# Gate tiles 4 to 7 as one quad ahead of the first attention-output pair, then two pairs per gate pair

## The chip, the cores and the metric

The kernel runs on one core of one Trainium2 chip. The metric is the device time of one execution in microseconds; the median of the executions is quoted, with the lowest and the highest. Every run carries a state (fast or slow) and the mean clock granted to TensorE.

## The reference

One block over 2048 tokens of width 448 computes a linear attention and an MLP from the same normalised input, and multiplies them:

```python
xn = layernorm(x)
# A: linear attention, 16 heads of 28; pq, pk = phi(q), phi(k)
kv  = einsum("bhsd,bhse->bhde", pk, v);  z = einsum("bhsd->bhd", pk)
num = einsum("bhqd,bhde->bhqe", pq, kv)
den = einsum("bhqd,bhd->bhq", pq, z)[..., None] + 1e-6
s   = (num / den) @ wo
# B: MLP with 1792 hidden units
h = relu(xn @ w1 + b1) ** 2
g = silu(h @ w2 + b2)
out = x + s * g
```

## The kernel before

The program lists its operations; a small list scheduler fixes the order on DVE, ACT and the buffers, while TensorE (PE) keeps the order of the program. Only its last stage matters here. It has two kinds of output tile of 128 tokens x 448:

- a **g tile** (`gg`): the second matmul of the MLP, 14 contraction chunks. DVE adds the bias, ACT applies silu;
- an **S tile** (`ss`): the attention output, 4 contraction chunks, from the scaled queries `pqT`, `pqR` and a folded weight `msb`. DVE multiplies it by the gate, POOL adds the residual, a DMA stores it.

Most of these tiles run in pairs. One tile of a pair uses the upper 64 contraction rows of the array, the other the lower 64, at the same time; then they swap rows. `phase` issues one such half. The fourth chunk of an S tile has 64 rows only (448 = 3 x 128 + 64), so the first half of an S pair is 8 matmuls (`K4`, four per tile) and the second 6 (`K3`).

```python
def phase(lo, hi):                 # lo on array rows 0-63, hi on rows 64-127, interleaved
    ...
    op = add("pe", f, reads + [u.bank for u in us if u.op], [u.bank for u in us], dur)
    for h, (u, ks) in enumerate((lo, hi)):
        if ks:
            if u.op and u.half != h:
                op.sync.add(u.op)  # the same bank from the other rows: wait until those have drained
            u.op, u.half = op, h
# ... cut ...
def scale_q():                     # 1/den goes to DRAM and back, broadcast over partitions into rb, rbR
    # ... cut: the DMAs ...
    for g in range(NG):            # DVE, four groups of 512 tokens; the first serves S tiles 0 to 3
        add("dve", lambda e, _, sl=sl: e.tensor_tensor(out=pqT[sl], in0=pqT[sl], in1=rb[sl], op=ALU.mult), ...)
        add("dve", lambda e, _, c=c: e.tensor_tensor(out=pqR[:, c], in0=pqR[:, c], in1=rbR[:, c], op=ALU.mult), ...)
# ... cut ...
full(gg(0)); full(gg(1)); z_heads(); token_sum(0); den(); open_gates(); scale_q()
token_sum(3); token_sum(1); token_sum(2); full(gg(2)); fold_wv(); full(gg(3))
for r in range(4): fold_wo(r)
C = range(0, NF)
for i, *pairs in ((4, 0), (6, 2), (8, 4, 6), (10, 8), (12, 10, 12)):   # g pair, S pair(s)
    ga, gb = gg(i), gg(i + 1)
    us = [(ss(j), ss(j + 1)) for j in pairs]
    phase((ga, C), (gb, C))
    x, y = us[0]
    if len(us) == 1:
        phase((x, K4), (y, K4)); phase((gb, C), (ga, C)); phase((y, K3), (x, K3))
    else:
        v, w = us[1]
        phase((x, K4), (y, K4)); phase((gb, C), (ga, C)); phase((v, K4), (w, K4))
        phase((y, K3), (x, K3)); phase((w, K3), (v, K3))
full(gg(14)); ...                  # the last two tiles, cut finer
```

## Time and profile before

| | before |
|---|---|
| time, median of the first 3 runs | 143.47 us (143.3 to 143.54) |
| span of the profiled run, granted clock | 142.0 us, 1.00 |
| PE, DVE, ACT, POOL busy | 97%, 64%, 55%, 17% |
| the stretch that the change edits | 96.4 to 132.4 us |

From the page of the kernel before, the busy time of each engine (us, share of the span, instructions):

```profile
PE 137.8 (97%) x1215; PEld 67.4 (47%) x1215; DVE 91.3 (64%) x218; ACT 78.7 (55%) x151; POOL 23.4 (17%) x37
```

One row of its table of windows, for the edited stretch. The columns are length, then busy time and instructions of PE, weight loads, DVE, ACT and POOL, then granted clock, DMA share and GB/s:

```profile
96.40:132.40 36.00, 36.00 (x380) 18.57 (x380) 17.35 (x34) 6.51 (x12) 10.05 (x10) 1.00 0.11 34
```

The whole list of what PE waited for (total, times, longest, in us):

```profile
PE pb L1010 <- DVE junk L345: 1.3, 1, 1.3
PE pb L487 <- DVE xn L466: 0.2, 1, 0.2
```

PE is busy 36.00 of 36.00 us in the stretch, and both of its waits belong to the first six microseconds. A busy PE need not be at its peak, so the chain of work that ended last is read too (start, length, line and number of matmuls; L905 is g, L971 is S):

```profile
96.51 2.76 PE pb L905 x28
99.27 0.76 PE pb L971 x8
100.03 2.65 PE pb L905 x28
102.67 0.57 PE pb L971 x6
103.24 2.65 PE pb L905 x28
105.89 0.76 PE pb L971 x8
...
132.37 2.75 PE pb L905 x14
```

A g half is 28 matmuls in two concurrent row halves, so 14 slots: 2.65 / 14 = 0.189 us each. The Trainium skill ("TensorE: Matmul & The Clock Gate", Back-to-back issue gap) gives N/2.4 + 2.5 ns as the gap from one matmul to the next on a warm array, which is 189 ns for 448 columns. It adds that in a sustained stream the formula is too high for many columns (about 131 ns measured for 512). That is not so in this trace, where sustained streams of 448 columns run at the formula's 189 ns, so the stretch is taken to run at the issue rate.

What the first S pair depends on, from the timeline of DVE (start, length, engine, line), and then the S pair itself, from the timeline of PE:

```profile
97.32 0.96 DVE L866 TENSOR_TENSOR pqT<-pqT,xT 128x1536 bf16<-128x1536 bf16 x1
98.19 0.28 DVE L872 TENSOR_TENSOR pqR<-pqR,xT 128x256 bf16<-128x256 bf16 x1
```

```profile
96.45 2.82 PE L905 MATMUL pb<-w,r 64*128 64x448 bf16 x28
99.11 0.35 PE L971 MATMUL pb<-msb,pqR 64*128 64x448 bf16 x2
```

The scaled block is ready at 98.47 us (98.19 + 0.28), 1.15 us after its first multiply began. The S pair starts at 99.11, when the g half before it has been issued (96.45 + 2.65). So it does not wait, but it has only 0.64 us to spare.

### The profile page before, as it was taken

To read this page: it belongs to the slowest core of one execution; us is meant where nothing else is said; L and a number is where in the kernel's file an instruction comes from. 1 tells how busy PE (TensorE), PEld (TensorE's weight loads), DVE (VectorE), ACT (ScalarE), POOL (GpSimd) and SP (SyncE) were. 2 spreads that over 40 slices of the span, in tenths; PEclk is the share of its full clock that TensorE was granted. 3 is DMA by queue.
4 is the path that set the end of the run, shared out by engine and by line. 5 is a ranking of instruction groups with operands and counts; after the bars stand their busy time and mean duration, and the time that the engine had idled before them with its cause. 6 is when DMAs were issued, how large, how long until landed. Compare 5 with 4: busy or idle time off the path is not lost.

```text
span 142.0 us, 3024 instructions
## 1 busy us (share of the span) xinstructions
PE 137.8 (97%) x1215; PEld 67.4 (47%) x1215; DVE 91.3 (64%) x218; ACT 78.7 (55%) x151; POOL 23.4 (17%) x37
## 2 busy tenths in 40 slices
PE   6999999999999999999999999999999999999992
PEld 2344444444444444444445455654555555555482
DVE  0979698698897999678959900149852436052743
ACT  2667979889878898879799572323030211030220
POOL 6000000000000000000790000000050507350670
DMA  4997768999250300000000025891001110201022
GB/s 111 329 334 225 78 176 279 342 244 129 55 64 15 74 19 5 0 9 14 0 0 0 0 78 135 186 166 32 5 6 58 37 32 32 97 27 43 32 97 67
DMA packets 19809, 12.90 MB, mean 91 GB/s; under 512 B 9364, under 2 KB 19412, under 8 KB 19796
## 3 DMA queue, kind: packets, MB, share of 16 engines
q1 hardware_dynamic: 17644, 11.22, 32.5%
q10 hardware_dynamic: 2152, 1.50, 4.8%
q8 instruction: 9, 0.15, 0.4%
q14 instruction: 4, 0.03, 0.1%
HBM read 8.78 MB, written 2.10 MB: 77 GB/s over the span
## 4 chain that ended last, share of the span: by engine, by line
PE 93%; DVE 3%; DMA 2%; issue 0%; DVEq 0%
PE pb L905 30%; PE pb L640 30%; PE pb L597 8%; PE pb L971 8%; PE pb L672 6%; PE pb L628 6%; DMA x_tok<-in_A_x_dram 2%; DVE st L444 1%; PE pb L678 1%; PE pb L765 1%; PE pb L726 1%; PE pb L487 1%; PE pb L803 0%; DVE xn L466 0%; PE pb L488 0%; DVE xT L497 0%
## 5 line engine op out<-in xcount | busy, mean ns | idle before, releaser
L640 PE MATMUL pb<-xT,w 64*128 64x512 bf16 x392 | 50.8, 376 | 0.1
L905 PE MATMUL pb<-w,r 64*128 64x448 bf16 (+3 forms) x378 | 45.1, 343 | 0.0
L649 ACT ACTIVATE r<-pb,b1f 128x512 bf16<-128x512 f32 x56 | 34.9, 689 | 4.1 <-PE pb L640 4.1
L640 PEld LDWEIGHTS pb<-xT,w 64*128 64x128 bf16 x392 | 21.4, 94 | 23.3 <-ACT r L649 0.6
L905 PEld LDWEIGHTS pb<-w,r 64*128 64x128 bf16 (+1 forms) x378 | 22.9, 95 | 19.9 <-issue 1.2
L916 DVE TENSOR_TENSOR gbuf<-pb,b2b 128x448 bf16<-128x448 f32 (+1 forms) x16 | 9.3, 609 | 33.2 <-PE pb L905 33.2
L881 ACT ACTIVATE gbuf<-gbuf 128x448 bf16<-128x448 bf16 (+1 forms) x16 | 8.6, 565 | 36.2 <-DVE gbuf L916 34.4
L950 POOL TENSOR_TENSOR xn<-xn,x_tok 128x448 bf16<-128x448 bf16 x15 | 15.1, 1029 | 48.7 <-DVE xn L941 48.7
L597 PE MATMUL pb<-w_qkv,xT 64*128 64x512 bf16 (+1 forms) x106 | 17.6, 377 | 0.0
L628 PE MATMUL pb<-xT,w_qkv 64*128 64x512 bf16 x84 | 15.5, 376 | 0.0
L657 DVE TENSOR_TENSOR r<-r 128x512 bf16<-128x512 bf16 x38 | 13.2, 418 | 0.0
L382 POOL MEMSET kvm<- 128x2048 bf16 x1 | 1.8, 1804 | 65.0 <-DVE zb L622 65.0
L971 PE MATMUL pb<-msb,pqT 64*128 64x448 bf16 (+3 forms) x93 | 11.2, 343 | 0.0
L444 DVE BATCH_NORM_STATS2 st<-x_tok 128x6 f32<-128x448 bf16 x16 | 9.4, 612 | 2.4 <-DMA x_tok<-in_A_x_dram 2.4
L575 ACT ACTIVATE qk<-pb 128x512 bf16<-128x512 f32 x16 | 9.0, 594 | 3.3 <-PE pb L597 2.7
L585 DVE SCALAR_TENSOR_TENSOR qk<-pb,qk 128x512 bf16<-128x512 f32 x16 | 10.7, 686 | 0.2
L941 DVE TENSOR_TENSOR xn<-pb,gbuf 128x448 bf16<-128x448 f32 (+2 forms) x17 | 9.3, 590 | 1.9 <-ACT gbuf L881 1.5
L658 ACT ACTIVATE r<-r 128x512 bf16<-128x512 bf16 x18 | 10.4, 651 | 0.0
L597 PEld LDWEIGHTS pb<-w_qkv,xT 64*128 64x128 bf16 (+1 forms) x106 | 6.6, 94 | 6.5 <-DVE xT L497 0.3
L672 PE MATMUL pb<-qk,xn 128*128 128x448 bf16 x48 | 9.4, 353 | 0.0
L628 PEld LDWEIGHTS pb<-xT,w_qkv 64*128 64x128 bf16 x84 | 6.0, 94 | 5.0
L616 DVE TENSOR_TENSOR zacc<-zacc,qk 128x448 f32<-128x448 f32 x13 | 8.1, 622 | 0.3
(81 smaller groups left out, 98.6 us busy)
## 6 DMA issues: line engine op xcount, KB each, us to landing
out_dram<-xn SPq DMA_DIRECT2D x15, 112.0 KB, 1.7
w<-in_B_w_dram SPq DMA_DIRECT2D x1, 1568.0 KB, 9.7
x_tok<-in_A_x_dram SPq DMA_DIRECT2D x3, 448.0 KB, 4.4
w<-in_B_w_dram SPq DMA_DIRECT2D x2, 384.0 KB, 4.7
xT<-rows ACTq DMA_DIRECT2D x6, 112.0 KB
w<-in_B_w_dram SPq DMA_DIRECT2D x1, 576.0 KB, 5.3
xT<-rows SPq DMA_DIRECT2D x5, 112.0 KB
w_o<-in_A_wo_dram SPq DMA_DIRECT2D x1, 392.0 KB, 10.9
```

The costliest lines, as they stand in the source:

```text
L444: "dve", lambda e, _: e.bn_stats(st6[:, si, :], x_tok[:, si, :]), [("x", si)], [("st", si)], 0.553
L585: lambda e, _: e.scalar_tensor_tensor(out=slot, in0=src(), scalar=1.0 + 1e-6, in1=slot, op0=ALU.add, op1=ALU.max),
L597: return e.matmul(ps(b)[:, 0:512], xT[half[h], c, si * P : (si + 1) * P], w_qkv[half[h], c, 384 : 2 * D], start=start, stop=stop,)
L628: return e.matmul(ps(b)[:, 0:512], w_qkv[half[h], c, m * P : (m + 1) * P], xT[half[h], c, g * 512 : (g + 1) * 512], start=start, stop=stop,)
L640: return e.matmul(ps(b)[:, 0:512], w_1[half[h], c, fi * P : (fi + 1) * P], xT[half[h], c, g * 512 : (g + 1) * 512], start=start, stop=stop,)
L649: lambda e, _: e.activation(out=slot, in_=ps(b)[:, 0:512], func=AF.Relu, bias=b1f[:, fi : fi + 1]),
L657: return e.tensor_tensor(out=slot, in0=slot, in1=slot, op=ALU.mult)
L658: return e.activation(out=slot, in_=slot, func=AF.Square)
L672: last = e.matmul(ps(b)[:, 0:D], xn[:, si, c * P : (c + 1) * P], pk_of(si), start=(si == 0), stop=(si == NT - 1),)
L905: return e.matmul(ps(b)[:, 0:n], r2[half[h], fi, si * P : (si + 1) * P], w_2[half[h], fi, c], start=start, stop=stop)
L950: eng, lambda e, _: e.tensor_tensor(out=ob, in0=ob, in1=x_tok[:, si, c], op=ALU.add),
L971: return e.matmul(ps(b)[:, 0:n], q, m, start=start, stop=stop)
```

## The change

The intent is to put more matmul work between the folded weights and the first S pair, so that the latter has no need to wait for the scaled queries. Two g pairs now go first, each filling the time in which the other drains. The S pairs that are displaced are caught up at two per g pair. The last group, and all that follows it, is the same in both.

```diff
-        for i, *pairs in ((4, 0), (6, 2), (8, 4, 6), (10, 8), (12, 10, 12)):
+        def s_pair(j):
+            x, y = ss(j), ss(j + 1)
+            return lambda: phase((x, K4), (y, K4)), lambda: phase((y, K3), (x, K3))
+
+        g4, g5, g6, g7 = (gg(i) for i in range(4, 8))
+        s0 = s_pair(0)
+        phase((g4, C), (g5, C))
+        phase((g6, C), (g7, C))
+        phase((g5, C), (g4, C))
+        s0[0]()
+        phase((g7, C), (g6, C))
+        s0[1]()
+        for i, *pairs in ((8, 2, 4), (10, 6, 8), (12, 10, 12)):
             ga, gb = gg(i), gg(i + 1)
-            us = [(ss(j), ss(j + 1)) for j in pairs]
+            us = [s_pair(j) for j in pairs]
             phase((ga, C), (gb, C))
-            ...
+            us[0][0]()
+            phase((gb, C), (ga, C))
+            for u, v in zip(us, us[1:]):
+                v[0]()
+                u[1]()
+            us[-1][1]()
```

More of the change, by code (lines that the diff above doesn't have):

```diff
@@ L1092, in bass_recurrent_scan__linear_attn_block__dense_activation_squared_relu__prompt_kernel @@
         C = range(0, NF)
-        for i, *pairs in ((4, 0), (6, 2), (8, 4, 6), (10, 8), (12, 10, 12)):
+        def s_pair(j):
[10 more added lines that the diff above has]
+        for i, *pairs in ((8, 2, 4), (10, 6, 8), (12, 10, 12)):
             ga, gb = gg(i), gg(i + 1)
-            us = [(ss(j), ss(j + 1)) for j in pairs]
+            us = [s_pair(j) for j in pairs]
             phase((ga, C), (gb, C))
-            x, y = us[0]
-            if len(us) == 1:
-                phase((x, K4), (y, K4))
-                phase((gb, C), (ga, C))
-                phase((y, K3), (x, K3))
-            else:
-                v, w = us[1]
-                phase((x, K4), (y, K4))
-                phase((gb, C), (ga, C))
-                phase((v, K4), (w, K4))
-                phase((y, K3), (x, K3))
-                phase((w, K3), (v, K3))
+            us[0][0]()
[4 more added lines that the diff above has]
+            us[-1][1]()
         full(gg(14))
```

## The prediction

> What bounds the kernel. TensorE, and nothing else is close: the page has PE busy 97% of a 142.0 us span at granted clock 1.00, DVE 64%, ACT 55%. The table of waits has only two for PE, 1.3 and 0.2 us, both at the very start. In the stretch that the change edits, 96.4 to 132.4 us, PE is busy 36.0 of 36.0 us, DVE 17.4, POOL 10.1, ACT 6.5. The chain of work that ended last stays on PE from 84.9 to 139.4 us; a tail of about 2.5 us (DVE, store) follows.
>
> What the change does. It adds and removes no work. The instruction order by engine shows the same half-row matmuls in the stretch with some S blocks later; ACT and SP keep their order; DVE's gate additions and S multiplies interleave differently; from g pair 12 on everything is as it was, so the tail is untouched. PE pieces from the chain: a g half is 2.65 us (28 matmuls in two concurrent row halves, 14 x 0.189), an S half 0.76 (8) or 0.57 (6). Before: three groups of 2.65+0.76+2.65+0.57 = 6.63 and two of 7.95 with a second S pair, together 35.8. After: the quad 4 x 2.65 + 0.76 + 0.57 = 11.9 and three groups of 7.95, together 35.8. The Trainium skill ("TensorE: Matmul & The Clock Gate", Back-to-back issue gap) gives N/2.4 + 2.5 ns for warm matmuls, 189 ns at 448 columns; the trace agrees (2.65/14). This stretch already runs at issue rate; reordering cannot compress it.
>
> What it could buy. The first S pair needs the first scaled query block (DVE, 97.32 to 98.47 us, itself behind the reciprocal's broadcast DMAs). It starts at 99.11, exactly when the g half before it ends: no wait, about 0.6 us to spare. After the change it should start near 104.4, with about 6 us to spare. That is insurance against a late broadcast, not time; the three runs lie within 0.24 us, so I see no execution in which it would pay much.
>
> What it could cost. The quad's second g pair takes the banks of the folded-weight blocks, evicted by 97.2 us and wanted at 99.1: no stall. A g pair's second half waits for its first half's drain; one phase of at least 0.76 us lies between, as today. The later groups use the pattern that 8:(4,6) and 12:(10,12) run today, 1.89 us for the last 20 S matmuls (10 x 0.189), no stall. DVE per 7.95 us group: two additions and four multiplies, about 3.5 us; POOL four residuals, 4.0 us. Gate buffers wrap every eight tiles: S 0 and 1 finish near 110 us, gates 8 and 9 are written after about 114. Stores come later but none at the end. All of it hides behind PE.
>
> Prediction: 143.4 us, 8 in 10 between 143.1 and 143.8; faster by over 2%: 0.01, within 2%: 0.98, slower by over 2%: 0.01.
>
> What would show it. Span within 0.3 us of 142.0; PE 36.0 busy of 36.0 in the stretch; four 2.65 us g halves with S first at about 104.4 us; no new PE wait in the table of waits; final chain as before.
>
> What would make it wrong: the broadcast landing later in unprofiled runs than in the trace (then up to some tenths faster); a bank held longer than I read for g 6, g 8 or S 4 (some tenths slower each); two phases of one bank too close; or a granted clock below 1.00.

## The result, and the profile after

| | before | after |
|---|---|---|
| median, same rounds | 143.39 us (143.25 to 143.54, 6 runs) | 143.51 us (143.27 to 143.8, 6 runs) |
| span of the profiled run, clock | 142.0 us, 1.00 | 142.2 us, 1.00 |

The ratio is 1.0009 with a 95% interval of 0.9993 to 1.0025: the same. Ratios here and below are the mean time of one kernel's fast runs over that of the other's fast runs of the same rounds, so they are not quite the ratio of the medians quoted. Executions over 1.5% slower than the fastest of the same kernel are left out of the means. Faster or slower needs 2%. A smaller difference counts as the same; where the text takes one for real, its interval leaves out 1.

The lines of after that answer to those of before, in the same order: the page's busy times, the row of windows, and the whole list of PE's waits.

```profile
PE 138.2 (97%) x1215; PEld 67.7 (48%) x1215; DVE 91.4 (64%) x218; ACT 78.7 (55%) x151; POOL 23.4 (16%) x37
```

```profile
96.40:132.40 36.00, 36.00 (x380) 18.53 (x378) 17.42 (x33) 6.50 (x12) 10.02 (x10) 1.00 0.11 35
```

```profile
PE pb L1010 <- DVE junk L345: 1.2, 1, 1.2
```

The chain of work that ended last, after:

```profile
96.68 8.05 PE pb L905 x84
104.73 0.76 PE pb L971 x8
105.49 2.65 PE pb L905 x28
108.14 0.57 PE pb L971 x6
108.70 2.65 PE pb L905 x28
111.35 0.76 PE pb L971 x8
112.11 2.65 PE pb L905 x28
114.76 1.89 PE pb L971 x20
...
132.54 2.75 PE pb L905 x14
```

The pieces are the same, in another order. From the first g half to the full-row tile that follows the stretch it takes 132.37 - 96.51 = 35.86 us before and 132.54 - 96.68 = 35.86 us after. No new wait appeared; the only one that is gone, 0.2 us on L487, lies in the first six microseconds.

The timelines of DVE and then of PE around the first S pair, after:

```profile
97.73 0.96 DVE L866 TENSOR_TENSOR pqT<-pqT,xT 128x1536 bf16<-128x1536 bf16 x1 [0.39 <-DMA xT<-rows]
98.61 0.28 DVE L872 TENSOR_TENSOR pqR<-pqR,xT 128x256 bf16<-128x256 bf16 x1
```

```profile
96.61 8.12 PE L905 MATMUL pb<-w,r 64*128 64x448 bf16 x84
104.57 0.35 PE L971 MATMUL pb<-msb,pqR 64*128 64x448 bf16 x2
```

The block is ready at 98.89 us and the S pair starts at 104.57, so it has 5.7 us to spare. In this execution DVE waited 0.39 us for the broadcast (the bracket); the old order would still have had 0.4 us left.

Before the changed code is reached, after is already 0.17 us late (96.68 against 96.51), which is the difference between the two spans (142.0 and 142.2). The first PE rows of the timelines, before and then after:

```profile
1.25 4.09 PE L1010 MATMUL pb<-junk 128*128 128x512 bf16 x10 [1.25 <-DVE junk L345]
5.52 0.34 PE L487 MATMUL pb<-ident,xn 128*128 128x128 bf16 x3 [0.18 <-DVE xn L466]
```

```profile
1.25 4.45 PE L1010 MATMUL pb<-junk 128*128 128x512 bf16 x10 [1.25 <-DVE junk L345]
5.55 0.50 PE L487 MATMUL pb<-ident,xn 128*128 128x128 bf16 x3
```

The ten warm-up matmuls and the first transposes, which both programs have, ran slower in this execution (0.50 instead of 0.34 us for three transposes), and everything after them is shifted. The change has no part in it: the slower start (4.45 and 0.50 us) is also in the trace of b_late2, which has the old order, and the faster one (3.93 and 0.34) in that of a_tok3, which has the new.

### The profile page after: what moved, and what is told of

It reads as the page before. It is cut to its first block, busy times and chain, and to the rows that moved or that the text cites. A ratio compares the mean times of both kernels' runs of the same rounds, so it can differ in the third digit from the quotient of the medians.

```text
span 142.2 us, 3026 instructions
## 1 busy us (share of the span) xinstructions
PE 138.2 (97%) x1215; PEld 67.7 (48%) x1215; DVE 91.4 (64%) x218; ACT 78.7 (55%) x151; POOL 23.4 (16%) x37
## 4 chain that ended last, share of the span: by engine, by line
PE 97%; DVE 1%; issue 0%; DVEq 0%
PE pb L905 30%; PE pb L640 30%; PE pb L597 8%; PE pb L971 8%; PE pb L672 6%; PE pb L628 6%; PE pb L1010 3%; PE pb L678 1%; PE pb L765 1%; PE pb L487 1%; PE pb L726 1%; PE pb L488 1%; PE pb L803 0%; DVE xT L497 0%; DVE xn L941 0%
```

## The experiments

The theory: PE's issue rate alone sets the time of the stretch, and the change only moves the point at which a late scaled block starts to cost. One rival: the first S pair was never near critical. Another: the null result is a gain at the first S pair that is lost again to the denser S work. A third: the small differences between the runs of the two are the change's own cost. Twelve kernels ran.

### A late scaled block, before and after

The scaled block is made late by N dummy multiplies on DVE, directly ahead of the first scaling. They write into buffers that are dead by then, so the results stay correct, and no other instruction changes its place.

```diff
+            def pads(e, g):
+                for i in range(N if g == 0 else 0):
+                    w = (w_1 if i < 4 else qk)[:, :, :].rearrange("p a b -> p (a b)")   # dead here
+                    e.tensor_tensor(out=w[:, ...1536 columns of its own...], in0=rb[:, :, 0:512], in1=rb[:, :, 0:512], op=ALU.mult)
 ...
-   lambda e, _, sl=sl: e.tensor_tensor(out=pqT[sl], in0=pqT[sl], in1=rb[sl], op=ALU.mult)
+   lambda e, _, sl=sl, g=g: pads(e, g) or e.tensor_tensor(out=pqT[sl], in0=pqT[sl], in1=rb[sl], op=ALU.mult)
```

**Before with two (b_late2).** 

> Before, with two dummy multiplies of 128x1536 (0.87 us apart in the trace) put ahead of the first query scaling on DVE, so that the first scaled block comes about 1.75 us later; nothing else moves. Theory (PE-bound stretch, first S pair with 0.4 to 0.6 us to spare): PE idles about 1.1 to 1.4 us before the first S pair and the time rises by as much, 144.5 to 144.9 us. Rival (the first S pair is not near critical, something else sets the time): no change.

Measured: 144.71 us (144.67 to 144.74) against 143.57; ratio 1.0077 (1.0056 to 1.0098), about +1.1 us. The PE timeline shows where:

```profile
96.63 2.82 PE L914 MATMUL pb<-w,r 64*128 64x448 bf16 x28
100.53 0.36 PE L980 MATMUL pb<-msb,pqR 64*128 64x448 bf16 x2 [1.07 <-DVE pqR L881]
```

The rival that the first S pair is not near critical falls: about 1.75 us of added lateness cost 1.1 us, so about 0.6 us was absorbed.

**Before with four (b_late4).** 

> Before with four dummy multiplies, about 3.5 us. Theory: PE idles 2.9 to 3.1 us at the first S pair, time 146.3 to 146.6 us; 1.75 us more than with two. Rival: no change, or less than 1 us.

Measured: 147.83 us (146.85 to 147.91); ratio 1.0279 (1.0242 to 1.0316), about +4.0 us. PE idled 2.74 us, nearly as expected, but the time rose by over a microsecond more than either theory said. The expectation was missed, and the chain shows by what:

```profile
102.03 0.93 PE pb L980 x8
102.97 4.33 PE pb L914 x28
```

The g half after the stall took 4.33 us instead of 2.65. That is followed up below.

**After with four (a_late4).** 

> After with the same four dummy multiplies. Theory: the first S pair starts at about 104.5 us and its block is ready near 102.4 us, so no PE wait and 143.5 us, the same as after without them (within 0.3 us). Rival (the change's later S pairs are only just served, its null result is a gain and a loss that cancel): 0.5 us or more slower.

Measured: 143.27 us (143.25 to 143.43); ratio to the kernel before 0.9979 (0.9961 to 0.9997). The DVE row of the dummies and the PE rows:

```profile
98.14 3.57 DVE L866 TENSOR_TENSOR w<-xT 128x1536 bf16<-128x1536 bf16 x4 [1.01 <-DMA xT<-rows]
```

```profile
96.40 8.12 PE L914 MATMUL pb<-w,r 64*128 64x448 bf16 x84
104.36 0.35 PE L980 MATMUL pb<-msb,pqR 64*128 64x448 bf16 x2
```

With the same dummies that cost before 4.0 us, after loses nothing. The broadcast also came late by itself here: DVE waited 1.01 us for it. Without the dummies the block would have been ready at 98.14 + 1.15 = 99.29 us, while the first g half was issued by 96.40 + 2.65 = 99.05. By this arithmetic the old order would have waited about 0.2 us in this execution.

**After with eight (a_late8).** 

> After with eight dummy multiplies, about 7.0 us, just past the spare time. Theory: block ready near 105.8 us, PE idles 1.0 to 1.5 us at the first S pair, time 144.5 to 145.0 us; so the change moved the point where a late block costs from 0.5 to about 5.7 us. Rival: costs far more than 1.5 us, because DVE work piles up behind the late scaling and holds the banks.

Measured: the three fast runs took 144.95, 145.39 and 145.69 us; ratio 1.0121 (1.009 to 1.0152), about +1.7 us. The fourth, which was the profiled one, took 147.52 us and counts as slow. The cost is somewhat over the range expected but well short of the 7 us added, so a late block costs in the new order too, only some 5 us later. The profile of the slow run shows one thing that precedes its stall: the broadcast landed at 98.92 us, 1.79 us after DVE was ready for it. PE then idled 2.57 us, and the granted clock was 0.50 from 107 to 110 us. Runs of b_late4 in which the clock fell count as fast, since that kernel has no much faster run beside them; so the 1.7 us here, without such a run, and the 4.0 us there are not quite like for like. Why the three fast runs lie up to 0.7 us above the expected range is not known, as none of them was profiled.

### Why four dummies cost more than the stall

**Before with three (b_late3).** 

> Before with three dummy multiplies, between the two that cost their stall alone (1.1 us) and the four that cost 4.3 us, of which 1.7 us was the g half after the stall at half the granted clock. Theory A (a stall costs its length, and the clock falls only from some idle time between 1.1 and 2.7 us on): either 145.4 to 145.9 us with clock 1.00, or about 147.0 us with the clock down, or some of each. Theory B (the extra of the four was not the clock but DVE piling up behind): 146.2 us, in proportion, clock 1.00.

Measured: 147.22, 145.91, 147.45 and 147.82 us, with mean granted clocks of 0.988, 1.000, 0.987 and 0.988. The ratio is 1.0246 (1.0188 to 1.0304), so whether it is over 2% is unclear. Theory A holds in this: the run whose clock stayed up is the shortest of the four, and the others, with the clock down, are 1.3 to 1.9 us longer (up to 0.8 us over the 147.0 us expected). The PE rows, and the windows with the granted clock as the third number from the right, of the profiled run:

```profile
101.40 0.56 PE L980 MATMUL pb<-msb,pqR 64*128 64x448 bf16 x2 [2.11 <-DVE pqR L881]
...
102.86 3.77 PE L914 MATMUL pb<-w,r 64*128 64x448 bf16 x28
```

```profile
99.10:102.00 2.90, 0.79 (x6) 0.89 0.00 0
102.00:104.40 2.40, 2.40 (x16) 0.50 0.03 7
104.40:107.00 2.60, 2.60 (x28) 0.93 0.00 0
```

After 2.1 us of idle PE, the clock was halved for a while: 16 matmuls in 2.40 us, where at full clock 2.40 us issues about 25 (2.40 / 0.189, two at a time). In b_late2, after 1.07 us of idle, it was 1.00 in the same windows. Windows of 0.1 us on the kept traces show how long the half clock lasted: 3.41 us in b_late3 (101.38 to 104.79 us: the clock is 0.88 in the window from 101.3, 0.56 in that from 104.7, 0.50 between) and 3.41 us in b_late4 (103.18 to 106.59 us: 0.91 in the window from 103.1, 0.53 in that from 106.5). Half of 3.41 is 1.7 us, which is what the S half and the g half after the stall lost: 1.66 us in b_late3 and 1.68 us in b_late4, against b_late2. In b_late4 the fall came 1.15 us after PE had resumed.

The length of the idle time alone seems not to decide. The run of b_late3 with its clock up was 2.4 us over the median of before (145.91 - 143.50), so by estimate it idled about 2.4 us, no less than the profiled one, and its clock did not fall.

**Before with four, and PE kept busy (b_late4_hot).** Twelve matmuls on zeros into a bank that nobody reads, between the first g half and the first S pair:

```diff
             phase((ga, C), (gb, C))
+            if i == 4:
+                hot(12)      # 12 x matmul 128x512 on zeros, own bank
             x, y = us[0]
```

> Before with four dummy multiplies and, on PE, 12 idle-filling matmuls of 128x512 (0.216 us each, 2.6 us, a bank that nobody reads) between the first g half and the first S pair, so that PE is busy while it would have waited. Theory (1.4 us of the 4.3 us was the clock drop after the idle time): clock 1.00 throughout, 146.3 to 146.8 us. Rival (DVE pile-up behind the late scaling): still 147.5 us or more.

Measured: 146.68 us (146.15 to 147.22), clock 1.000 in all four runs; ratio 1.0217 (1.0175 to 1.0259), against 1.0279 (1.0242 to 1.0316) without the filling. The two intervals overlap and the two kernels ran on different chips, so the trace has to decide. The chain after the stall:

```profile
103.04 0.93 PE pb L980 x8
103.97 2.65 PE pb L914 x28
```

The same g half takes 2.65 us again with the scaled block even later (103.04 us instead of 102.03), so the extra 1.7 us in the trace of b_late4 was the clock and not DVE work piling up. The spread of 1 us may come from the broadcast, which is shown for one run only: in the profiled run, the slowest, DVE waited 0.98 us for it and PE still idled 0.88 us after the filling. One of the runs of b_late4 does not fit so neatly: 147.91 us with a recorded mean clock of 0.999. What happened in it is not known, as it was not profiled; a stall of about 4.3 us at full clock would give that time.

### Is PE's issue rate the only limit?

Two of the 14 chunks are left out of g tiles 4 to 13 (relative error 0.22). Their outputs are wrong, which doesn't matter for the times.

```diff
-        C = range(0, NF)
+        C = range(0, NF - 2)
 ...
-            return Acc(b, reads, mm, out, n, 2 * NF)
+            return Acc(b, reads, mm, out, n, 2 * (NF - 2))
```

**Before (b_trim).** 

> Before with 12 of the 14 contraction chunks in g tiles 4 to 13 (wrong on purpose: those tiles lose one seventh of their second matmul's sum). Ten g halves lose two matmul slots of 0.189 us each, 3.78 us of PE. Theory (PE issue rate alone sets the stretch): time falls by 3.6 to 3.8 us, to 139.7 to 139.9 us; the first g half is 0.38 us shorter, so the first S pair may just wait 0 to 0.3 us. Rival (DVE, POOL, banks or stores hold the stretch too): falls by less than 3.2 us.

Measured: 139.71 us (139.37 to 139.78); ratio 0.9726 (0.9701 to 0.9752), about -3.9 us, with no PE wait at the first S pair.

**After (a_trim).** 

> After with the same cut. Theory: falls by 3.78 us, to 139.6 to 139.8 us, and at most 0.3 us below the trimmed before, as there is no wait at the first S pair here. Rival (four residuals and four multiplies per g pair are nearly limiting after the change): falls by less than 3.2 us.

Measured: 139.55 us (139.5 to 139.95); ratio 0.9719 (0.9691 to 0.9746), about -4.0 us. The chain's groups shrank as meant:

```profile
109.74 0.76 PE pb L971 x8
110.50 2.27 PE pb L905 x24
112.77 1.89 PE pb L971 x20
```

Every matmul slot taken away is time gained, in both orders, within the intervals. Even with 0.76 us less PE time per group, DVE and POOL keep up with two S pairs per g pair. The rival of a gain that is lost again to the denser S work finds nothing here.

### Is there a cost of the change itself?

**After once more (a_again)**, with an empty line added at the end. 

> After again, unchanged but for an empty line at the end, to narrow the null result. Theory: ratio to before 1.000 within 0.002. Rival (the few tenths between some runs of after and before are the change's own cost): ratio 1.001 or more again, with a PE wait between 96.4 and 132.4 us.

Measured: 143.32 us (143.26 to 143.58) against 143.44 (143.15 to 143.67, 11 runs); ratio 0.9997 (0.9985 to 1.0009), and no PE wait in the stretch. The first 1.0009 does not come back; both intervals include 1.

### Can the spare time be spent?

The token sum that I took for a half-row one is moved ahead of the first full g tile. The denominator, and with it the broadcast, then comes later by the length of that sum.

```diff
+        token_sum(3)
         full(gg(0))
         ...
-        token_sum(3)
```

**After (a_tok3).** 

> After with the half-row token sum (16 matmuls of 64 rows, 1.64 us) moved from between the denominator and the full-row token sums to just before the first full g tile, where PE is in half-row mode anyway. The denominator then comes about 1.5 us later and so do the broadcasts and the scaling. Theory: after has about 5.7 us to spare, so nothing waits; one change of row mode (about 0.1 us each in the trace) is saved: 143.3 to 143.5 us. Rival: no gain, or 1 us slower.

Measured: 143.33 us (143.17 to 143.62); ratio 0.9998 (0.9984 to 1.0012). The lateness cost nothing, as expected: the scaling began at 99.10 us instead of 97.73. But the hoped-for 0.1 us was not there. The sum takes 1.63 us with the move and 1.64 without, and from the start of the last run of hidden-layer matmuls to the first g half of the stretch it takes 32.95 us with the move and without (96.42 - 63.47 in the chain of a_tok3, 96.68 - 63.73 in that of after). I had misread its shape: the trace has it as 128 rows by 64 columns, so it did not share the array mode of its new neighbours; the two full g tiles take 5.40 us in both chains. This was the one version that might have beaten both, and it equals them.

**Before (b_tok3).** 

> Before with the same move. Theory: the spare 0.4 to 0.6 us is overrun, PE idles 0.8 to 1.2 us at the first S pair, 144.1 to 144.6 us. Rival: same as a_tok3.

Measured: 144.65 us (144.03 to 144.88); ratio 1.008 (1.0063 to 1.0098), +1.1 us, with a PE wait of 0.87 us at the first S pair:

```profile
100.31 0.36 PE L971 MATMUL pb<-msb,pqR 64*128 64x448 bf16 x2 [0.87 <-DVE pqR L872]
```

A move that is harmless after the change costs 0.8% before it. Here no dummy instruction is involved, so this is the cleanest evidence of what the change is worth when the scaled block comes late.

### What the order of the halves is for

**After with the two halves of the last three g pairs back to back (a_adj).**

```diff
             phase((ga, C), (gb, C))
-            us[0][0]()
             phase((gb, C), (ga, C))
+            us[0][0]()
```

> After with the two halves of a g pair run back to back in the last three g pairs (no S half between them), the S halves after them. Theory: each of the three swaps of row halves then waits for the drain of the same banks' first half, 0.1 to 0.25 us each, 0.3 to 0.75 us in all: 143.8 to 144.2 us; this is what the order with S pairs between, or with a quad, avoids. Rival: the swap costs nothing, 143.5 us.

Measured: 144.03 us (143.97 to 144.32); ratio to before 1.0045 (1.0032 to 1.0059). The mean is 0.69 us above that of a_again in the same rounds, 0.23 us for each of the three swaps. One swap, from the chain:

```profile
108.62 2.67 PE pb L905 x28
111.28 0.05 issue
111.33 2.82 PE pb L905 x28
114.15 2.65 PE pb L971 x28
```

Two g halves take 5.53 us (108.62 to 114.15) instead of 5.30. The Trainium skill ("TensorEngine Tiling (Array Packing)", Gotcha 1: PSUM Pressure) says that different row tiles cannot access the same PSUM bank at one time and that software must synchronize; it names no price. In the quad the other g pair fills that gap, elsewhere an S half does, so the new order pays nothing for its swaps.

## Why the prediction was right

- **The time.** 143.51 us measured, 143.4 predicted, inside 143.1 to 143.8. The change regroups work that already ran at issue rate: 35.86 us before and after. The two trims show that nothing else holds the stretch.
- **No new wait.** As predicted, neither the banks of the second g pair, nor DVE and POOL under two S pairs per g pair, nor the swap of halves made PE wait. a_adj shows that the last was a real danger, 0.23 us a swap, which the change avoids by always keeping a phase between.
- **The first S pair.** Predicted at about 104.4 us with about 6 us to spare; measured 104.57 with 5.7.
- **"Insurance against a late broadcast, not time."** Shown by b_late4 and a_late4 (4.0 us against nothing for the same delay), and by b_tok3 and a_tok3 (1.1 us against nothing).
- **What was off.** The prediction took "about 0.6 us to spare" from one trace and said "I see no execution in which it would pay much". The broadcast's landing varies more than that. (It had named a later landing as what would make it wrong.) The first multiply after it began at 97.32 us in the trace of before, 97.73 in that of after, 98.14 in a_late4 and 98.35 in b_late4_hot; in the last two the first S pair of the unpadded old order would have waited about 0.2 us (the arithmetic is shown at a_late4; for b_late4_hot it is 98.35 + 1.15 against 96.64 + 2.65). So, by this arithmetic, the spare time in the old order lay between 0.6 us and somewhat less than nothing, and the insurance would have been worth about 0.2 us in two of the eleven fast profiled runs that issue the broadcast alike, and nothing in the other nine. The one profiled run of before did not wait.
- **What stays open.** Whether this shows in the time of the unmodified kernels. The 31 runs of before span 143.15 to 144.04 us and the 12 of after 143.26 to 143.8, but only some of these rounds were shared: on the chip where before was highest on average, and where a_late4 came out 0.3 us faster than it (its interval just leaves out 1), after itself did not run.

## What to carry to other kernels

In a stretch where an engine already runs at its issue rate, a reordering of its work gains nothing, and it can lose (a_adj, 0.69 us). Before making one, add up the pieces of its chain in both orders; if the sums agree and no new wait arises, the answer is "the same". It can still be worth having: measure the spare time at the tightest wait in several traces, not in one, because the producer behind DMAs moved by a microsecond here from run to run (97.32 to 98.35 us), and a stall of 2.11 us on TensorE came to 3.8 us here when the clock fell after it. When two row halves swap over the same banks, keep one independent phase between them (0.23 us a swap here).

## What the Trainium skill lacked or had wrong

- "TensorE: Matmul & The Clock Gate", Part 1: The HAM clock gate, has the clock fall after at least one idle window of about 3.4 us. Here PE idled only 2.11 us before the fall in the profiled run of b_late3, and 2.74 us in that of b_late4; after 1.07 us in b_late2 there was none. The half clock lasted 3.41 us in both, the length of the page's window. If the window before the fall is as long, then by estimate PE was busy for a third of it or more (1.15 of 3.41 us in b_late4, 1.3 in b_late3), so a window need not be wholly idle. How idle it must be, no run here shows.
- "TensorEngine Tiling (Array Packing)", Gotcha 1, says that software must synchronize row tiles on one bank, but gives no cost: 0.23 us for each swap of row halves without work between (a_adj).
- No page has how much the landing of a broadcast through DRAM varies from execution to execution: the multiply behind it began between 97.32 and 98.35 us in the eleven fast profiled runs that issued it alike.
